# Load order ahead of the last weight-gradient blocks, the shift gradient's row by band products, and a last block in column halves

## The chip, the cores and the metric

The kernel runs on one core of a Trainium2 chip. The metric is device time in microseconds (us) of one execution, taken as the median of several runs. The engines are called PE (matrix products, with PEld for its weight loads), ACT, DVE and POOL (elementwise work, copies, small operations), and SP (issues transfers). Transfers that SP issues form one queue in program order; POOL issues another, and ACT a few.

## What is computed

The program runs a four-layer forward pass and its backward pass, and returns the output and eight gradients. Cut to what the change touches:

```python
def _A_ref(q, k, v, shift_k, ssm_k, ssm_D):      # S=2048, D=448, ks=4
    k_pad = jnp.pad(k, ((0, 0), (ks - 1, 0), (0, 0)))
    for t in range(ks):
        k_shift = k_shift + k_pad[:, t:t + S, :] * shift_k[:, ks - 1 - t][None, None, :]
    kv = k_shift * v
    ...                                            # long convolution of kv with ssm_k, by FFT
    return q * (y + kv * ssm_D)
def _B_ref(x, w1, w2):                             # w1: [448, 1792], w2: [1792, 448]
    h = silu(einsum("bsd,df->bsf", x, w1))
    return einsum("bsf,fd->bsd", h, w2)
x = x + _A_ref(layernorm(x), ...); x = x + _B_ref(layernorm(x), ...)
x = x + _A_ref(layernorm(x), ...); x = x + _B_ref(layernorm(x), ...)
# returned: x, and the gradients of q, k, v, shift_k, ssm_k, ssm_D, w1, w2
```

Three of the gradients matter here. The one of `w2` ([1792, 448], output 8) and the one of `w1` ([448, 1792], output 7) are sums over the 2048 rows and over both dense layers. The one of `shift_k` ([448, 4], output 4) holds, for each of the 448 channels and 4 shifts, one sum over the rows.

## The kernel before

The first 460 us or so run the tiled forward and backward passes. They write to DRAM what the weight gradients need: the activations `A0_d`, `A1_d`, the gradients `GH0_d`, `GH1_d` (one for each of the two dense layers) and the normalised rows `N_d` (two tensors, one for each layer). The rest is class `Tail`: `jobs("w2")`, an FFT stage, `ends` (gradients of k, v, ssm_k, ssm_D and shift_k) and `jobs("w1")`. The work of these parts is interleaved on PE.

**Order.** No engine's order is written by hand. Each step is recorded with `s.op(cost, fn, r, w, prio, ...)`: its guessed cost on each engine it may run on, the tiles that it reads and writes, a priority (lower goes first), for a transfer also kind and bytes, and `behind`, a list of steps after whose issue it may be issued. `Sched.plan` (a list scheduler with guessed rates, `RATE`) turns this into one order for every engine, and the program is emitted in that order. Semaphore waits come from the tiles: a reader waits for the writer, a writer waits for the readers of the buffer that it takes over. The guessed costs and rates only decide order.

**Weight gradients, `jobs`.** The 1792 columns are cut into seven blocks p = 0..6 of 256 columns, each of two halves u = 0, 1 of 128. For a block, both layers' operands (gi = 0, 1) of 16 row tiles are loaded into an operand buffer `jb` [128, 16, 256] of 1024 KB; then each half sums 2 x 16 matmuls (stationary: `jb`, 128x128; moving: 448 columns) into one PSUM tile `ps_d`. There are three `jb` buffers, and for w1 every even block's first operand (p = 0, 2, 4, 6, gi = 0) is kept in the buffer of `Minv` where `(2p + gi) % 4 == 0`; the buffer `Minv` is free when the last `ps_gK` and `ps_gkv` products are done. For `w2` the operand is a plain load from `A0_d`/`A1_d` (L1114); for `w1` it is a transposing load from `GH1_d` and `GH0_d` (L1112), and the moving operand is `nmov`, the rows `N_d[1]` and `N_d[0]`, loaded in two halves each (L1095, 896 KB each). All are issued by SP. In step p = 1 of w1 both halves share one two-bank PSUM tile. A copy `dob` of `ps_d` to SBUF follows (L92 on ACT, L94 on DVE); blocks 0 to 5 are transposed by a transfer (L1191) and stored by POOL (L1208, L1210). Block 6 is transposed by PE (`ps_dt`, L1197, four products per half), copied (`do`), and stored by SP in one transfer (L1212), which ends the program.

The last 2 x 448-column sums of w2 (block 6) come directly before block 0 of w1. The order of SP's queue there is: second-last w2 operand, rows `N_d[1]` (2 loads), last w2 operand, first transposing load of GH1, rows `N_d[0]` (2 loads), second transposing load, and so on.

**Shift gradient, `ends`.** For each group q of 128 channels (64 in the last), 32x128 products `ps_sk` (L1051, two halves h of 8 row tiles) hold on their diagonal the wanted sums. DVE multiplies with an identity (`gsel`, L1061), reduces (`gsk`, L1063, one value per channel and shift) and casts into `gskb` (L1065). PE turns `gskb` into one row on one partition by 16 transposes (`ps_gs`, L1075), ACT copies it in another order (`gsr`, L1079), and POOL stores it (L1080). Interleaved on DVE are the sums `gka`/`gkp` (L1027 to L1036) of the gradient of k, in eight steps g, each stored by POOL (L1039).

Of the kernel before, what the change touches and what calls it, by code (L numbers as in the profile page):

```python
# [20 lines left out]
P = 128  # L21
S = 2048
D = 448
# [109 lines left out]
class Sched:  # L133
# [5 lines left out]
    STEP = 20  # L139
    RATE = {"plain": 300e3, "turn": 160e3, "load": 190e3, "rows": 220e3}  # L140

# [18 lines left out]
    def at(self, base, *key):  # L160
        return base + NUDGE.get(key, 0.0)
# [188 lines left out]
def _pm(ap2d):  # L350
    return ap2d.rearrange("(p j) d -> p j d", j=J)
# [487 lines left out]
class Tail:  # L839
# [119 lines left out]
    def ends(self, pr):  # L959
# [63 lines left out]
        for g in range(8):  # L1023
# [15 lines left out]
            s.op({"POOL": 0.6}, lambda e, gk=gk, g=g: nc.gpsimd.dma_start(out=out2[:, 2 * g:2 * g + 2, :], in_=gk[:]), r=[gk], prio=pr + 5, dma=("plain", 230e3))  # L1039
        gskb = s.vb("P2", "gskb", [P, 4, 4], BF16, "gskb")  # L1040
        prev = []
        for q in range(4):
# [15 lines left out]
            def pick(e, q=q, nb=nb, pd=pd, sel=sel, gsk=gsk):  # L1058
                for b in range(nb):
                    m = k.ident[32 * b:32 * b + 32, 32 * b:32 * b + 32].unsqueeze(1)  # L1060
                    nc.vector.tensor_tensor(out=sel[32 * b:32 * b + 32], in0=pd[32 * b:32 * b + 32], in1=m.to_broadcast([32, 4, 32]), op=ALU.mult)  # L1061
                n = 32 * nb
                nc.vector.tensor_reduce(out=gsk[0:n], in_=sel[0:n], axis=mybir.AxisListType.X, op=ALU.add)  # L1063
                for j in range(4):
                    nc.vector.tensor_copy(gskb[0:n, q, j:j + 1], gsk[0:n, 3 - j:4 - j])  # L1065

            s.op({"DVE": 1.5}, pick, r=[pd], w=[sel, gsk, gskb], prio=pr + 4)

        pg = self.unit([1, 4, D], BF16, "ps_gs")

        def row4(e):
            for q in range(4):
                n = 128 if q < 3 else 64
                for j in range(4):
                    nc.tensor.transpose(pg[0:1, j, 128 * q:128 * q + n], gskb[0:n, q, j:j + 1], k.ident[0:n, 0:n])  # L1075
# [4 lines left out]
        s.op({"POOL": 0.6}, lambda e: nc.gpsimd.dma_start(out=k.outs[4].rearrange("(o d) j -> o (d j)", o=1), in_=gsr[:]), r=[gsr], prio=pr + 4, dma=("plain", 5e3))  # L1080

    def jobs(self, which, pr):
        nc, s, k = self.nc, self.s, self.k
        if which == "w2":
            gm = s.vb("res", "W1", [P, NT, D], BF16, "gmov")
            gs = [gm.sub() for _ in range(4)]
            gl = [lambda i=i: s.op({"SP": 0.4}, lambda e: nc.sync.dma_start(out=gm[:, 4 * i:4 * i + 4, :], in_=_pm(k.grad_out[0])[:, 4 * i:4 * i + 4, :]), w=[gs[i]], prio=pr - 30, dma=("plain", 458e3), behind=[k.lastA_op]) for i in range(4)]
            groups = [("A1", [gs[t // 4] for t in range(NT)], lambda t: gm[:, t, :]), ("A0", k.G2v, lambda t: k.G2[:, t, :])]
        else:
            nm = [s.vb("PF", ("A1", "B1v")[i], [P, NT, D], BF16, "nmov") for i in range(2)]  # L1090
            nh = [[v.sub() for _ in range(2)] for v in nm]
            for i in (1, 0):
                for h in range(2):
                    hs = slice(8 * h, 8 * h + 8)
                    s.op({"SP": 0.4}, lambda e, i=i, hs=hs: nc.sync.dma_start(out=nm[i][:, hs, :], in_=_pm(k.N_d[i][:])[:, hs, :]),  # L1095
                         r=[k.st_[("n", i, j)] for j in range(8 * h, 8 * h + 8)], w=[nh[i][h]], after=self.done[i], prio=pr - 30 if i else pr + 0.5, dma=("plain", 917e3), behind=k.loads[-1 - i:][:1])
            groups = [("GH1", [nh[1][t // 8] for t in range(NT)], lambda t: nm[1][:, t, :]), ("GH0", [nh[0][t // 8] for t in range(NT)], lambda t: nm[0][:, t, :])]
# [29 lines left out]
        else:  # L1127
            for p, gi, at in ((0, 0, pr), (1, 0, pr + 0.2), (0, 1, pr + 1), (1, 1, pr + 2)):
                bring(p, gi, 0, 16, at)
        for p in range(NF // 2):  # L1130
            q = s.at(pr + 12.5 * p, p, which)
# [25 lines left out]
            if (which, p) == ("w1", 1):  # L1157
                prev = first[:4]
            both = True
            steps = [(u, gi) for gi in range(2) for u in range(2)] if both else [(u, gi) for u in range(2) for gi in range(2)]  # L1160
# [3 lines left out]
            for x, (u, gi, ts) in enumerate(split):  # L1164
                ends = [[y for y in range(len(split)) if split[y][0] == u][z] for z in (0, -1)]
# [4 lines left out]
                def mm(e, ts=ts, gi=gi, u=u, rows=rows, ps=pss[u], at=groups[gi][2], first=(x == ends[0]), last=(x == ends[1])):  # L1170
                    for t in ts:
                        nc.tensor.matmul(ps[:, :D], lhsT=rows(t, gi, u), rhs=at(t), start=(first and t == ts[0]), stop=(last and t == ts[-1]))  # L1172

                if (which, p, x) == ("w1", 1, 4):
                    prev = [first[-1], mine[-1]]
                prev = [s.op({"PE": 0.19 * len(ts)}, mm, r=[*[parts[gi][t] or k.lastA for t in ts], *[groups[gi][1][t] for t in ts]], w=[pss[u]], prio=q + 0.05 * x - (12.35 if (which, p) == ("w1", 1) and x < 4 else 0), after=prev + (self.last if p else [k.lastG] if u and which == "w2" else []))]
# [5 lines left out]
            for u in range(2):  # L1182
                ps = pss[u]
# [4 lines left out]
                s.op({"ACT": 0.55, "DVE": 0.62}, lambda e, ps=ps, ob=ob: _copy(nc, e, ob[:], ps[:, :D]), r=[ps], w=[ob], prio=q)  # L1188
# [6 lines left out]
                def tr(e, ob=ob, pt=pt):  # L1195
                    for dc in range(ND):
                        nc.tensor.transpose(pt[:, dc, :], ob[:, dc * DC:(dc + 1) * DC], k.ident[:])  # L1197

                s.op({"PE": 0.25}, tr, r=[ob], w=[pt], prio=q)
                s.op({"ACT": 0.6, "DVE": 0.4}, lambda e, pt=pt, o=o, u=u: _copy(nc, e, o[:, :, u, :], pt[:]), r=[pt], w=[o], prio=q)  # L1200
            if which == "w2":
# [13 lines left out]
def kernel(  # L1215
# [68 lines left out]
    "P1": dict(pq=3, sp=1),  # L1284
    "P2": dict(skb=1, gK=2, gkv=2, gKD=1, sel=2, gsk=2, gskb=1, gKr=1, oo=2, ob=2),
}
# [100 lines left out]
```

## Time and profile before

| what | before |
|---|---|
| median of 3 runs (lowest to highest) | 700.63 us (699.21 to 701.17) |
| the profiled execution: its time | 699.83 us |
| its span, first to last instruction | 698.0 us |
| PE, DVE, ACT, POOL busy in the span | 97%, 73%, 58%, 24% |
| granted PE clock | 1.00 of full speed in every stretch from 566 to 696 us |

PE is close to always busy, so a saving counts when it shortens PE's own sequence, a wait of PE, or the few steps after PE's last product. The chain of waits is read backwards from the last instruction: it names, at each step, what released it. A row of the timeline reads: start, duration, engine, line, operation, tile written and read, shapes, count, and in square brackets how long the engine had stood idle before it and what ended that. For SP and POOL a transfer's row is its issue, not its landing; landings are in the view of transfers.

### The profile page before, as it was taken

Reading aid. Unit: us, or ns where it says so; the run is one execution under the profiler, and the core shown is the slowest. Engines: PE = TensorE matmul, PEld = TensorE weight load, DVE = VectorE, ACT = ScalarE, POOL = GpSimd, SP = SyncE. Lnnn points to the kernel's source line nnn. Section 1 sums busy time; section 2 is a strip of 40 time slices with the busy share of each in tenths; the row PEclk is TensorE's granted clock in tenths of the full one; section 3 lists DMA queues with packets and bytes.
Section 4 is the critical chain, followed back from the end, with each engine's and each line's share of the span. In section 5 each row is a group of like instructions: output and inputs, shape, how many; then the busy total and the mean of one; then the engine's idle time right before and its main releaser. Section 6 shows DMA issues by size and latency. Waiting matters only on the chain. (4 is left out here: it accounts for less than half of the span.)

```text
span 698.0 us, 18012 instructions
## 1 busy us (share of the span) xinstructions
PE 676.8 (97%) x7448; PEld 469.2 (67%) x7464; DVE 512.8 (73%) x1203; ACT 401.8 (58%) x486; POOL 168.2 (24%) x290
## 2 busy tenths in 40 slices
PE   6999898999999999999999999999999999999997
PEld 4887666776767776777767767655767765455553
DVE  5989798668889888888889877864699679951000
ACT  4989987776667556766567666425876550002001
POOL 1254153203222323122212201013143131102221
PEclk9999999999999999999999999999999999999999
DMA  9979988989788978787886769977699679999972
GB/s 320 289 247 291 363 165 181 199 180 190 181 154 180 183 189 181 177 176 187 183 181 143 174 158 237 296 191 231 201 387 350 181 258 302 302 238 219 230 159 46
DMA packets 280671, 151.86 MB, mean 218 GB/s; under 512 B 230159, under 2 KB 261631, under 8 KB 280205
## 3 DMA queue, kind: packets, MB, share of 16 engines
q1 hardware_dynamic: 265854, 108.29, 67.2%
q0 software_dynamic: 13968, 41.62, 19.5%
q8 instruction: 58, 0.95, 0.6%
q10 hardware_dynamic: 766, 0.80, 0.4%
q14 instruction: 25, 0.20, 0.1%
HBM read 50.68 MB, written 54.60 MB: 151 GB/s over the span
## 5 line engine op out<-in xcount | busy, mean ns | idle before, releaser
L1172 PEld LDWEIGHTS <-jb 128*128 128x128 bf16 x892 | 85.8, 98 | 81.6 <-DMA jb<-GH_d 2.0
L92 ACT CAST ghp<-ps_g 128x896 bf16<-128x896 f32 x64 | 58.1, 908 | 58.5 <-PE ps_g L672 48.5
L726 PE MATMUL ps_o<-w2sb,aT 128*128 128x448 bf16 x448 | 89.7, 352 | 0.8 <-ACT aT L700 0.8
L726 PE MATMUL ps_n<-w1T,ghT 128*128 128x448 bf16 x448 | 90.0, 352 | 0.0
L1172 PE MATMUL ps_d<-nmov,jb 128*128 128x448 bf16 x448 | 86.3, 353 | 2.2 <-DMA jb<-GH_d 1.6
L663 PE MATMUL ps_h<-nT,w1sb 128*128 128x128 bf16 x1344 | 85.6, 219 | 0.8 <-ACT nT L92 0.8
L663 PE MATMUL ps_g<-nT,w2T 128*128 128x128 bf16 x1344 | 85.7, 219 | 0.0
L663 PEld LDWEIGHTS <-w2T 128*128 128x128 bf16 x1344 | 77.3, 98 | 7.2
L663 PEld LDWEIGHTS <-w1sb 128*128 128x128 bf16 x1344 | 76.7, 98 | 5.2 <-issue 0.9
L726 PEld LDWEIGHTS <-aT 128*128 128x128 bf16 x448 | 43.0, 98 | 38.4 <-ACT aT L700 1.0
L726 PEld LDWEIGHTS <-ghT 128*128 128x128 bf16 x448 | 43.1, 98 | 37.8
L700 ACT ACTIVATE aT<-ps_h 128x896 bf16<-128x896 f32 x64 | 56.7, 916 | 19.9 <-PE ps_h L672 11.0
L622 POOL TENSOR_TENSOR rstd<-ve,mhalf 128x1 f32<-128x1 f32 x64 | 39.3, 614 | 106.6 <-DVE ve L619 106.6
L700 ACT ACTIVATE dT<-ps_h 128x896 bf16<-128x896 f32 x60 | 53.3, 915 | 14.9 <-PE ps_h L672 10.0
L750 DVE SCALAR_TENSOR_TENSOR junk<-u,n 128x448 bf16<-128x448 bf16 x64 | 39.9, 624 | 23.2 <-ACT u L829 22.2
L92 ACT CAST dob<-ps_d 128x448 bf16<-128x448 f32 x13 | 6.9, 532 | 70.9 <-PE ps_d L1172 70.9
L700 ACT ACT_TABLE_LOAD x36 | 46.2, 1283 | 1.2 <-issue 0.6
L1172 PE MATMUL ps_d<-G,jb 128*128 128x448 bf16 x224 | 45.7, 353 | 0.1
L1172 PE MATMUL ps_d<-gmov,jb 128*128 128x448 bf16 x220 | 45.1, 352 | 0.0
L617 DVE BATCH_NORM_STATS2 st<-x 128x6 f32<-128x448 bf16 x64 | 40.0, 625 | 1.5
L739 DVE TENSOR_TENSOR ghT<-ghp,dT 128x896 bf16<-128x896 bf16 x64 | 39.4, 620 | 1.1 <-ACT ghp L92 0.9
L829 ACT ACTIVATE u<-ps_n,rstd 128x448 bf16<-128x448 f32 x32 | 20.3, 636 | 32.3 <-POOL rstd L622 13.8
(180 smaller groups left out, 1218.2 us busy)
## 6 DMA issues: line engine op xcount, KB each, us to landing
A_d<-turned SPq DMA_DIRECT2D x32, 448.0 KB, 4.0
GH_d<-ghT SPq DMA_DIRECT2D x32, 448.0 KB, 4.1
jb<-A_d SPq DMA_DIRECT2D x12, 1024.0 KB, 6.7
KK<-KK POOLq DMA_DIRECT2D x14, 256.0 KB, 5.1
spec_K<-KK POOLq DMA_DIRECT2D x7, 512.0 KB, 6.0
spec_KV<-X POOLq DMA_DIRECT2D x7, 512.0 KB, 7.7
N_d<-n POOLq DMA_DIRECT2D x32, 112.0 KB, 4.0
sp_c<-spec_KV POOLq DMA_DIRECT2D x14, 256.0 KB, 6.6
```

Source lines behind the costliest of these rows:

```text
L92: nc.scalar.copy(out, in_)
L617: nc.vector.bn_stats(out=st[:], in_=x[:])
L622: s.op({"POOL": 1.0}, lambda e: nc.gpsimd.tensor_tensor(out=rs[:], in0=ve[:], in1=self.k.mhalf[:, 0:1], op=ALU.pow), r=[ve], w=[rs], prio=pr)
L663: nc.tensor.matmul(ps[:, i, :], lhsT=at(b, ft), rhs=nT[:, b, :], **f)
L700: prev = [s.op({"ACT": 0.93}, lambda e, i=i, fun=fun, out=out, late=late: nc.scalar.activation(out[:, 7 * i:7 * i + 7, :], c[:, 7 * i:7 * ...
L726: nc.tensor.matmul(po[:, :D], lhsT=a[:, ft, :], rhs=wt[:, ft * D:(ft + 1) * D], start=(ft == 0), stop=(ft == NF - 1))
L739: s.op({"DVE": 0.57}, lambda e, i=i, t=t: nc.vector.tensor_tensor(out=gh[:, 7 * i:7 * i + 7, :], in0=t[:], in1=d[:, 7 * i:7 * i + 7, :], o ...
L750: nc.vector.scalar_tensor_tensor(out=junk[:], in0=u[:], scalar=1.0, in1=n[:], op0=ALU.mult, op1=ALU.mult, accum_out=cp[:, 1:2])
L829: s.op({"ACT": 0.85}, lambda e: nc.scalar.activation(u[:], pn[:, :D], ACT.Identity, scale=r[:], accum_out=cp[:, 0:1]), r=[pn, r], w=[u, cp ...
L1172: nc.tensor.matmul(ps[:, :D], lhsT=rows(t, gi, u), rhs=at(t), start=(first and t == ts[0]), stop=(last and t == ts[-1]))
```

## The change

There are three edits, and one changed guess of a rate in the planner.

1. **Order of the loads** (`jobs("w1")`). The first transposing load of GH1 (p = 0, gi = 0) gets priority `pr - 60` and goes behind the second-last operand of w2 instead of behind the last; the row loads of both `N_d[1]` and `N_d[0]` go behind the last operand of w2; the other transposing loads go behind that one too.
2. **Shift gradient**. Two constant tiles are made on POOL (`spread`: four 32x32 identities below each other; `band`: ones in four bands). DVE spreads each channel's four sums over 32 columns (`gskx`, four multiplications of 128x32 per group instead of four casts of 128x1). Four matmuls with `band` as stationary operand sum them into a [14, 128] tile, in place of the 16 transposes; ACT copies that tile, and POOL stores 14 lines of 256 bytes instead of one row.
3. **The last block of w1** (p = 6). Half u = 1 is cut into two column halves of 224 with a PSUM tile each; copy, PE transposes and copy are done for each of the two (two `ps_dt` products instead of four).

In the built program, the order on PE before the last blocks changes too: the second half of the `ps_sk` products of group 1 moves from the middle of w2's block 6 to the middle of w1's block 0, the two `ps_sk` steps of group 3 move to within the last products of w1's block 1 and between the halves of block 2, and the four band products come after the first layer's products of block 2. On DVE the copy of one `ps_d` half at 641 us goes to ACT; on POOL the store of w2's block 6 moves ahead of the fourth `gkp` store. SP's queue becomes: second-last w2 operand, first transposing load of GH1, last w2 operand, rows `N_d[1]`, rows `N_d[0]`, second transposing load, and so on.

The diff, cut to its core:

```diff
-    RATE = {"plain": 300e3, "turn": 160e3, "load": 190e3, "rows": 220e3}
+    RATE = {"plain": 300e3, "turn": 160e3, "load": 215e3, "rows": 220e3}
...
+        spread = s.vb("P2", "m32", [P, 32], BF16, "gsm")
+        band = s.vb("P2", "band", [P, 4, 16], BF16, "gsl")
+        def masks(e):
+            nc.gpsimd.memset(band[:], 0.0)
+            for b in range(4):
+                nc.gpsimd.memset(band[32 * b:32 * b + 32].rearrange("p q r -> p (q r)")[:, b:b + 61:20], 1.0)
+                nc.gpsimd.tensor_copy(spread[32 * b:32 * b + 32], k.ident[32 * b:32 * b + 32, 32 * b:32 * b + 32])
+        s.op({"POOL": 1.5}, masks, w=[spread, band], prio=pr)
+        gskx = s.vb("P2", "gK", [P, 4, 32, 4], BF16, "gskx")
...
                 for j in range(4):
-                    nc.vector.tensor_copy(gskb[0:n, q, j:j + 1], gsk[0:n, 3 - j:4 - j])
+                    nc.vector.tensor_scalar(out=gskx[0:n, q, :, j], in0=spread[0:n], scalar1=gsk[0:n, 3 - j:4 - j], scalar2=None, op0=ALU.mult)
...
-        pg = self.unit([1, 4, D], BF16, "ps_gs")
-        def row4(e):
+        pg = self.unit([14, P], FP32, "ps_gs")
+        def lines(e):
             for q in range(4):
                 n = 128 if q < 3 else 64
-                for j in range(4):
-                    nc.tensor.transpose(pg[0:1, j, 128 * q:128 * q + n], gskb[0:n, q, j:j + 1], k.ident[0:n, 0:n])
+                nc.tensor.matmul(pg[:], lhsT=band[0:n, q, 0:14], rhs=gskx[0:n, q].rearrange("p e j -> p (e j)"), start=(q == 0), stop=(q == 3))
-        s.op({"PE": 1.0}, row4, r=[gskb], w=[pg], prio=pr + 4)
+        s.op({"PE": 0.25}, lines, r=[gskx, band], w=[pg], prio=pr + 4)
-        gsr = s.vb("P2", "gK", [1, D * 4], BF16, "gsr")
-        s.op({"ACT": 1.8}, lambda e: nc.scalar.copy(gsr[:].rearrange("o (d j) -> o j d", j=4), pg[:]), r=[pg], w=[gsr], prio=pr + 4)
+        gsr = s.vb("P2", "gsr", [14, P], BF16, "gsr")
+        s.op({"ACT": 0.2}, lambda e: nc.scalar.copy(gsr[:], pg[:]), r=[pg], w=[gsr], prio=pr + 4)
...
-            for i in (1, 0):
+            def rows_of(i, behind):
                 for h in range(2):
                     hs = slice(8 * h, 8 * h + 8)
...
-                         r=[k.st_[("n", i, j)] for j in range(8 * h, 8 * h + 8)], w=[nh[i][h]], after=self.done[i], prio=pr - 30 if i else pr + 0.5, dma=("plain", 917e3), behind=k.loads[-1 - i:][:1])
+                         r=[k.st_[("n", i, j)] for j in range(8 * h, 8 * h + 8)], w=[nh[i][h]], after=self.done[i], prio=pr - 30, dma=("plain", 917e3), behind=behind)
+            rows_of(1, k.loads[-1:])
+            rows_of(0, k.loads[-1:])
+            second = k.loads[-1]
+            k.load = k.loads[-2:-1]
...
-            for p, gi, at in ((0, 0, pr), (1, 0, pr + 0.2), (0, 1, pr + 1), (1, 1, pr + 2)):
+            for p, gi, at in ((0, 0, pr - 60), (1, 0, pr + 0.2), (0, 1, pr + 1), (1, 1, pr + 2)):
                 bring(p, gi, 0, 16, at)
+                if (p, gi) == (0, 0):
+                    k.load = [second]
...
+            cols = [(0, 0, D), (1, 0, D)]
+            if (which, p) == ("w1", NF // 2 - 1):
+                cols = [(0, 0, D), (1, 0, D // 2), (1, D // 2, D)]
+                pss.append(self.unit([P, 512], FP32, "ps_d"))
             if split is None:
-                split = [(u, gi, range(8 * h, 8 * h + 8)) for u, gi in steps for h in range(2)]
+                split = [(v, gi, range(8 * h, 8 * h + 8)) for gi in range(2) for v in range(len(cols)) for h in range(2)]
...
-                        nc.tensor.matmul(ps[:, :D], lhsT=rows(t, gi, u), rhs=at(t), start=(first and t == ts[0]), stop=(last and t == ts[-1]))
+                        nc.tensor.matmul(ps[:, c0:c1], lhsT=rows(t, gi, u), rhs=at(t)[:, c0:c1], start=(first and t == ts[0]), stop=(last and t == ts[-1]))
...
-                pt = self.unit([DC, ND, P], BF16, "ps_dt")
+                ds = range(c0 // DC, c1 // DC)
+                pt = self.unit([DC, len(ds), P], BF16, "ps_dt")
                 def tr(e, ob=ob, pt=pt, ds=ds):
-                    for dc in range(ND):
-                        nc.tensor.transpose(pt[:, dc, :], ob[:, dc * DC:(dc + 1) * DC], k.ident[:])
+                    for i, dc in enumerate(ds):
+                        nc.tensor.transpose(pt[:, i, :], ob[:, dc * DC:(dc + 1) * DC], k.ident[:])
```

More of the change, by code (lines that the diff above doesn't have):

```diff
@@ L1163, in jobs, with mm @@
             mine = []
-            for x, (u, gi, ts) in enumerate(split):
-                ends = [[y for y in range(len(split)) if split[y][0] == u][z] for z in (0, -1)]
+            for x, (v, gi, ts) in enumerate(split):
+                u, c0, c1 = cols[v]
+                ends = [[y for y in range(len(split)) if split[y][0] == v][z] for z in (0, -1)]
                 def rows(t, gi, u, p=p, early=early, st=st):
                     return k.lastA[:, 2 * p + u, :] if early and which == "w2" and (gi, t) == (0, 15) else st[gi][:, t, u * P:(u + 1) * P]
-                def mm(e, ts=ts, gi=gi, u=u, rows=rows, ps=pss[u], at=groups[gi][2], first=(x == ends[0]), last=(x == ends[1])):
+                def mm(e, ts=ts, gi=gi, u=u, rows=rows, ps=pss[v], c0=c0, c1=c1, at=groups[gi][2], first=(x == ends[0]), last=(x == ends[1])):
@@ L1181, in jobs @@
                 prev = [first[-1], mine[-1]]
-            for u in range(2):
-                ps = pss[u]
+            for v, (u, c0, c1) in enumerate(cols):
+                ps = pss[v]
                 if which == "w2":
@@ L1284 @@
     "P1": dict(pq=3, sp=1),
-    "P2": dict(skb=1, gK=2, gkv=2, gKD=1, sel=2, gsk=2, gskb=1, gKr=1, oo=2, ob=2),
+    "P2": dict(skb=1, gK=2, gkv=2, gKD=1, sel=2, gsk=2, m32=1, band=1, gsr=1, gKr=1, oo=2, ob=2),
 }
```

20 lines of the change are left out of this document (9 added, 11 removed).

## The prediction

> **What bounds the kernel now.** First I read the page: PE is busy nearly all of the span.
>
> ```profile
> span 698.0 us, 18012 instructions
> ...
> PE 676.8 (97%) x7448; PEld 469.2 (67%) x7464; DVE 512.8 (73%) x1203; ACT 401.8 (58%) x486; POOL 168.2 (24%) x290
> ```
>
> So a saving must shorten PE's own sequence, one of its waits, or the steps after its last product. All three edits act after 575 us, and in the built program every engine's order before that point is unchanged except for nine small POOL operations. Next I read the chain of waits in order of time from there on (start, duration, what):
>
> ```profile
> 594.54 14.78 DMA jb<-GH_d
> 609.36 1.69 PE ps_d L1172 x8
> ...
> 627.55 0.54 ACT dob L92
> 628.14 1.67 PE ps_d L1172 x8
> ...
> 638.70 0.96 PE ps_gs L1075 x16
> 639.66 51.56 PE ps_d L1172 x272
> ...
> 691.44 1.53 PE ps_d L1172 x8
> 692.99 0.54 ACT dob L92
> 693.58 0.45 PE ps_dt L1197 x4
> 694.05 0.42 DVE do L94
> ```
>
> Between 594 and 692 us PE loses time in two places only, and PE's timeline has their size in the brackets:
>
> ```profile
> 609.36 1.69 PE L1172 MATMUL ps_d<-nmov,jb 128*128 128x448 bf16 x8 [1.61 <-DMA jb<-GH_d]
> ...
> 628.14 1.67 PE L1172 MATMUL ps_d<-nmov,jb 128*128 128x448 bf16 x8 [0.62 <-ACT dob L92]
> ```
>
> PE waits 1.61 us for the second transposing load of GH1 and 0.62 us for a copy of half a block. After 628 it never waits until 693. At most about 2.2 us of waits, 1 us of `ps_gs` and a part of the end are to be had: a large gain is not there.
>
> **Edit 1, the order of the loads.** SP's queue and the landings of single issues:
>
> ```profile
> 574.85 0.52 SPq L1114 DMA_DIRECT2D jb<-A_d  x1
> 575.60 2.25 SPq L1095 DMA_DIRECT2D nmov<-N_d  x2
> 581.57 0.52 SPq L1114 DMA_DIRECT2D jb<-A_d  x1
> 582.27 11.07 SPq L1112 DMA_TRANSPOSE jb<-GH_d  x1
> 593.44 1.01 SPq L1095 DMA_DIRECT2D nmov<-N_d  x2
> 594.54 10.90 SPq L1112 DMA_TRANSPOSE jb<-GH_d  x1
> ...
> 631.91 4.76 SPq L1112 DMA_TRANSPOSE jb<-GH_d  x1
> ```
>
> ```profile
> jb<-A_d SPq DMA_DIRECT2D x1, 1024.0 KB, 10.4
> ...
> jb<-GH_d SPq DMA_TRANSPOSE x1, 14.8
> ```
>
> The load that PE waits for is issued at 594.54 and lands 14.8 later, at 609.3. In the changed order its issue can come at about 588 (its buffer is free when PE has used up the second operand of w2's block 5). But an earlier issue helps only if the DMA engines would otherwise idle. These are the windows (PE, PEld, DVE, ACT, POOL busy, clock, DMA share, GB/s):
>
> ```profile
> 582.00:584.00 2.00, 2.00 (x12) 1.02 (x11) 1.97 (x3) 0.00 (x0) 0.00 (x0) 1.00 0.99 409
> ...
> 590.00:592.00 2.00, 2.00 (x41) 1.07 (x40) 1.97 (x4) 0.00 (x0) 0.33 (x1) 1.00 1.19 100
> 592.00:594.00 2.00, 2.00 (x12) 1.06 (x11) 2.00 (x4) 0.00 (x0) 0.23 (x1) 1.00 1.27 290
> ...
> 598.00:600.00 2.00, 2.00 (x12) 1.02 (x11) 1.88 (x9) 0.53 (x1) 0.00 (x0) 1.00 1.07 421
> ...
> 602.00:604.00 2.00, 2.00 (x13) 0.99 (x12) 1.97 (x3) 0.27 (x1) 0.71 (x1) 1.00 0.74 82
> ```
>
> From 578 to 609 the engines are full, with two thin places, at 590 to 592 and 602 to 604: in each a transposing load comes to the head of the queue, and for some 1.5 us little flows. Between the issue at 574.85 and the landing at 609.3 the queue carries eight loads (two w2 operands, four halves of rows, two transposing loads); in the changed order the same eight stand up to and including the second transposing load, and two transposing loads still follow plain ones. So I expect its landing to move little. What does change is a POOL store. Here are the fourth `gkp` store and the store of w2's block 6:
>
> ```profile
> 596.95 0.54 POOL L1039 DMA_DIRECT2D out_dram<-gkp  x1 [4.71 <-DVE gkp L1036]
> 602.56 0.71 POOL L1202 DMA_DIRECT2D out_dram<-do  x1 [5.08 <-ACT do L92]
> ```
>
> They change places, so the 224 KB that were issued at 596.95 leave after 603; at 421 GB/s they take 0.5 us out of the way of the awaited load. PE needs it at the same point as before (same products ahead of it). The wait goes from 1.6 to 1.1: **-0.5**. Bounds: -1.6 (the wait vanishes, if the first load's thin 1.5 us falls behind the plain load then still in flight) and +2.8 above the present wait (the rival below).
>
> The first transposing load is moved past the last w2 operand and the rows `N_d[1]`, and holds SP meanwhile: its issue took 11.07 with four loads in front, and one such issue took 4.76 at 631.91 where none was. With one load in front I take about 8.5, an estimate from the flow: the plain load in front needs until about 580 (1024 KB at some 300 GB/s from 576.5), the transposing load some six more (a thin 1.5 us, then 1024 KB at the 290 of the window from 592, and a store), and SP is released some 2 us before the last of it (it was at 593.34, while the rate of rows comes after 595). So SP is free at 584, not 582. The last w2 operand then goes out about 2.5 us later and, with the 10.4 from issue to landing, lands by 594.5; PE asks for it at 594.8. The rows `N_d[1]`, needed at 601, go out 10 us later than now and land by about 597. Both stay hidden, the first barely. `N_d[0]` is needed at 616 only.
>
> **The order on PE.** The 0.62 wait comes from step p = 1, whose halves share one PSUM tile: the last eight products wait for the copy of the first half. In the changed order the 16 `ps_sk` products of group 3 stand between, and they cost the same anywhere:
>
> ```profile
> 629.81 0.55 PE ps_sk L1051 x16
> ```
>
> 0.55 of the 0.62 is covered: **-0.55** (bounds 0, if the products are held by the same copy, and -0.62). The second `ps_sk` step of group 1 moves from 596.4 to about 604.4. DVE's next step needs it:
>
> ```profile
> 598.26 1.19 DVE L1061 TENSOR_TENSOR gsel<-ps_sk,ident 32x128 f32<-32x128 f32 x4
> ...
> 635.61 0.57 DVE L1061 TENSOR_TENSOR gsel<-ps_sk,ident 32x128 f32<-32x128 f32 x2 [6.95 <-PE ps_sk L1051]
> ```
>
> DVE stands idle some 6 us there, and the four sums g = 4 to 7 queue behind it (also their stores). It has room: it stood idle 6.95 before the last `gsel`. That step then ends at about 634, while PE needs its result at about 636, 16 products after the last `ps_sk`. If DVE were another 6 us late, PE would wait 4; I take 0.
>
> **Edit 2, the band products.** Sixteen transposes take 0.96 on PE, in the chain. Four products of 128 columns take their place. The nearest rows are `ps_gK` with 128 columns and its own weights, and the transposes themselves:
>
> ```profile
> 558.37 0.89 PE ps_gK L1002 x16
> ```
>
> 0.89/16 = 0.056, 0.96/16 = 0.060: four cost 0.22 to 0.24. **-0.73**. On DVE four multiplications of 128x32 replace four casts; bounds are the casts and the 112x112 form:
>
> ```profile
> L414 DVE TENSOR_SCALAR KK<-ident,skc 112x112 bf16<-112x112 bf16 x16 | 2.6, 246 | 5.2 <-POOL skc L408 5.2
> ...
> L1065 DVE CAST gskb<-gsk 128x1 bf16<-128x1 f32 x12 | 1.0, 149 | 0.1
> ```
>
> At most 4 x 0.1 = 0.4 us per group, in the room just named. ACT's copy gets shorter, off the path. POOL's nine operations on the masks fall in its idle 9 us before the first `gK` store; at 0.1 to 0.3 each they need 1 to 3:
>
> ```profile
> 555.17 0.57 POOL L1007 DMA_DIRECT2D out_dram<-gK  x1 [9.04 <-ACT gK L92]
> ```
>
> ```profile
> L407 POOL MEMSET KK<- 112x32 bf16 x2 | 0.4, 300 | 0.0
> ```
>
> **Edit 3, the end.** 32 products of 448 columns become 64 of 224. Per product 51.56/272 = 0.190 in the chain for 448 columns and 0.056 for 128: on a straight line 0.096 for 224, so 64 x 0.096 - 32 x 0.190 = +0.1 (bounds 0 and +6, if a half cost as much as a whole; the 128-column row with its own weights excludes most of that). The Trainium skill (TensorE: Matmul & The Clock Gate, Part 1) puts a warm product at its columns over 2.4 GHz plus 2.5 ns, which is 95.8 ns here; by it the sum would be the same to 0.1. Two transposes more stand before the last products: +0.1. Behind them, ACT's copy shrinks from 448 to 224 columns:
>
> ```profile
> 560.21 0.91 ACT L985 CAST gkv<-ps_gkv 128x896 bf16<-128x896 f32 x1
> ...
> 689.79 0.53 ACT L92 CAST dob<-ps_d 128x448 bf16<-128x448 f32 x1 [8.59 <-PE ps_d L1172]
> ```
>
> 0.38 for 448 columns more, so 0.34 for 224: -0.19. Two transposes instead of four: 0.45 to 0.34, -0.11. The last copy has 256 columns on ACT (0.15 + 0.22 = 0.37) instead of 512 on DVE (0.42): -0.05. Sum of the end: **-0.15** (bounds -0.35 and +0.2).
>
> **Sum.** -0.5 - 0.55 - 0.73 - 0.15 = -1.9 us. The profiled execution took 699.83 (span 698.0 and 1.8 around it), so 697.9 in its frame. The three timed runs have the median 700.63, 0.8 above it; the mean of all four is 700.2. I subtract from that: 698.3, and say 698.4.
>
> **The rivals.**
> (a) The wait vanishes. For it: the thin 1.5 us of the first transposing load may fall under the plain load in front of it, and the store leaves the window. Against it: in both places before, plain loads were in flight too, and it was not hidden. -1.6 instead of -0.5: -3.0, 697.2.
> (b) Slower. The place is SP at 575.5: if the moved load holds SP for 11.07, as it did at 582.27, the last w2 operand is issued at 586.5, 5 us late, and lands at 596.9 (10.4 after issue); PE, which wants it at 594.8, waits 2.1. All loads behind are 5 late, so the second transposing load lands at 613.8 against a need at 609.9 and PE waits 3.9. Waits of 6.0 instead of 1.6 (+4.4), less the 1.4 of the other edits: +3.0, 703.2. It decides when SP is held beyond 584.4 (594.8 - 10.4), an issue of 9 us. For it: both issues quoted took 11. Against it: those had rows of 1.8 MB and more in front, this one has 1 MB. The Trainium skill (Advanced Engine Details and Errata, X-Bar Transpose (TRN2)) says that transposing transfers are as fast as plain ones; by it this rival could not arise and its chance would be nil, but the rows of 11.07 and 0.52 for the same 1024 KB do not agree.
> (c) The order does not do what it says: the landing stays, and the `ps_sk` products are held with the copy. Only -0.73 - 0.15 remain: -0.9, 699.3.
>
> **How the numbers follow.** Forecast 0.47, (a) 0.31, (b) 0.08, (c) 0.14. About 0.3% (2.1 us) is what a measurement of this kernel can tell from no change. The forecast's -1.9 lies just inside; with its own spread of about 1, I give 0.4 of it to faster. Faster: 0.31 + 0.19 = 0.50. Slower: most of (b), 0.06. Within: 0.44. The forecast's own range is 697.3 to 699.6; (a) and (c) and the spread of the runs (about 1 either way) widen it to 696.5 and 700.8, which leaves (b) out.
>
> **What would show it.** In the changed profile: PE's wait for `jb<-GH_d` near 608 of about 1 us (0: rival a; a wait at 594.8 before the `jb` of w2 as well: b); the first transposing issue at 575.5 holding SP 7 to 9 us; no PE wait over 0.2 for `dob` near 627; `ps_gs` x4 in about 0.25; from the last `ps_d` product to the last issue 1.25 us instead of 1.55 (692.99 to 694.5). I am wrong if PE waits anywhere for DVE's `gskx`, or if the 64 half products take over 6.3 us.

## The result and the profile after

| | before | after |
|---|---|---|
| median of the timed runs | 700.63 us (9 runs) | 698.38 us (9 runs) |
| ratio of after to before, 95% interval | | 0.9972 (0.9959 to 0.9986) |
| the profiled execution: its time, its span | 699.83, 698.0 us | 696.9, 695.1 us |

The changed kernel is 0.28% faster. The two profiled executions differ by 2.9, but 1.04 of that is there before the change acts: the second-last w2 operand is issued at 574.85 before and at 573.81 after. What is compared from here on is the **stretch** from that issue to the issue of the last output: 119.69 before (574.85 to 694.54), 117.84 after (573.81 to 691.65), so **-1.85**.

The chain of waits of the changed kernel (start, duration, what) where it differs:

```profile
607.89 1.69 PE ps_d L1192 x8
...
626.08 0.54 ACT dob L92
...
635.05 0.41 PE ps_gs L1084 x4
635.46 53.13 PE ps_d L1192 x304
...
688.82 0.77 PE ps_d L1192 x8
...
690.50 0.35 ACT dob L92
690.90 0.33 PE ps_dt L1219 x2
691.25 0.37 ACT do L92
```

`ps_gs` has shrunk from 0.96 to 0.41, and the steps behind the last product are 0.35, 0.33 and 0.37 long instead of 0.54, 0.45 and 0.42. PE's timeline at the two former waits:

```profile
607.89 1.69 PE L1192 MATMUL ps_d<-nmov,jb 128*128 128x448 bf16 x8 [1.18 <-DVE gka L1035]
...
625.98 0.62 PE L1061 MATMUL ps_sk<-kx_s,gks 128*32 128x128 bf16 x16
626.66 4.70 PE L1192 MATMUL ps_d<-nmov,jb 128*128 128x448 bf16 x24
```

The wait for the second transposing load is still there, 1.18 instead of 1.61. The bracket names a DVE step, because its end fell beside the landing. SP's queue and the landing show the true one: issue at 588.43, landing 19.4 later, at 607.8.

```profile
573.81 0.52 SPq L1129 DMA_DIRECT2D jb<-A_d  x1
574.55 7.68 SPq L1127 DMA_TRANSPOSE jb<-GH_d  x1
582.33 0.53 SPq L1129 DMA_DIRECT2D jb<-A_d  x1
583.04 5.30 SPq L1105 DMA_DIRECT2D nmov<-N_d  x4
588.43 15.32 SPq L1127 DMA_TRANSPOSE jb<-GH_d  x1
```

```profile
jb<-GH_d SPq DMA_TRANSPOSE x1, 19.4
```

(Where a run without the early stores, e6 below, has the same DVE step end at 609.7, PE passes this place at 608.5 without a wait: it doesn't wait for DVE.) At 626 the 16 `ps_sk` products fill the time of the copy `dob`: they end at 626.60, the copy at 626.62, and no bracket is left. The first moved load held SP for 7.68. DVE's two late steps:

```profile
603.63 1.19 DVE L1071 TENSOR_TENSOR gsel<-ps_sk,ident 32x128 f32<-32x128 f32 x4 [5.47 <-PE ps_sk L1061]
...
633.03 0.69 DVE L1075 TENSOR_SCALAR gskx<-gsm,gsk 64x32 bf16<-64x32 bf16 x4
```

DVE stood idle 5.47, and its last `gskx` was done at 633.7, 1.3 ahead of PE's use at 635.05. On POOL the two stores have changed places:

```profile
600.86 0.71 POOL L1224 DMA_DIRECT2D out_dram<-do  x1 [9.24 <-ACT do L92]
601.56 0.57 POOL L1039 DMA_DIRECT2D out_dram<-gkp  x1
```

The fourth `gkp` store landed at 607.4, 0.4 ahead of the second transposing load; before, it was issued at 596.95 and landed at 604.3, 5 ahead of that load.

### The profile page after: what moved, and what is told of

It is laid out like the page before. It is cut to its first block, busy times and chain, and to the rows that moved or that the text cites. A ratio compares the mean times of both kernels' runs of the same rounds, so it can differ in the third digit from the quotient of the medians.

```text
span 695.1 us, 18061 instructions
## 1 busy us (share of the span) xinstructions
PE 675.2 (97%) x7468; PEld 471.5 (68%) x7484; DVE 513.6 (74%) x1202; ACT 398.8 (57%) x489; POOL 169.5 (24%) x299
## 5 line engine op out<-in xcount | busy, mean ns | idle before, releaser
L1192 PEld LDWEIGHTS <-jb 128*128 128x128 bf16 x924 | 88.9, 98 | 77.9 <-DMA jb<-GH_d 1.6
L1192 PE MATMUL ps_d<-nmov,jb 128*128 128x448 bf16 (+1 forms) x480 | 86.5, 340 | 1.3 <-DVE gka L1035 1.2
L92 ACT CAST dob<-ps_d 128x448 bf16<-128x448 f32 (+1 forms) x15 | 7.6, 507 | 74.7 <-PE ps_d L1192 74.7
```

What stands on the lines that cost most here:

```text
L92: nc.scalar.copy(out, in_)
L1192: nc.tensor.matmul(ps[:, c0:c1], lhsT=rows(t, gi, u), rhs=at(t)[:, c0:c1], start=(first and t == ts[0]), stop=(last and t == ts[-1]))
```

## The experiments

The runs by the stretch and what PE lost in it (T2 is the wait for the second transposing load; "copy" is the half-block copy at 627; "other" are waits for other loads; "clock" is what products took longer while the granted PE clock was 0.50, explained at e4; the rest is the stretch less these). e5 moves the issue at which the stretch starts and is left out.

| kernel | stretch | T2 | copy | other | clock | rest |
|---|---|---|---|---|---|---|
| before | 119.69 | 1.61 | 0.62 | - | - | 117.46 |
| after | 117.84 | 1.18 | - | - | - | 116.66 |
| e9, after again, timed | 117.87 | 1.21 | - | - | - | 116.66 |
| e8, after again | 120.21 | 1.95 | - | - | 1.59 | 116.67 |
| e7, bands in reverse | 117.84 | 1.17 | - | - | - | 116.67 |
| e1, old order | 120.16 | 2.88 | 0.62 | - | - | 116.66 |
| e2, old order, one store less | 119.26 | 0.95 | 0.62 | 0.85 | - | 116.84 |
| e3, new order alone | 118.16 | 0.61 | - | - | - | 117.55 |
| e4, rows `N_d[0]` late | 123.99 | - | - | 4.63 | 2.80 | 116.56 |
| e6, after, four stores less | 116.50 | - | - | - | - | 116.50 |
| e10, rows `N_d[1]` first | 117.75 | - | 0.62 | 0.43 | - | 116.70 |
| e11, both rows first | 124.89 | - | - | 5.54 | 2.70 | 116.65 |
| e12, half of them first | 117.98 | 1.43 | - | - | - | 116.55 |

This table is the main reading. With bands and halves the rest is 116.5 to 116.8 in eleven profiles, without them 117.46 and 117.55: edits 2 and 3 are worth 0.8 to 0.9 wherever they stand. All else is waits, and in three runs the clock after a wait. Edit 1 moves only those.

### e1: the old order, bands and halves kept

```diff
-            rows_of(1, k.loads[-1:])
-            rows_of(0, k.loads[-1:])
-            second = k.loads[-1]
-            k.load = k.loads[-2:-1]
+            for i in (1, 0):
...
-                         ... prio=pr - 30, dma=("plain", 917e3), behind=behind)
+                         ... prio=pr - 30 if i else pr + 0.5, dma=("plain", 917e3), behind=k.loads[-1 - i:][:1])
...
-            for p, gi, at in ((0, 0, pr - 60), (1, 0, pr + 0.2), (0, 1, pr + 1), (1, 1, pr + 2)):
+            for p, gi, at in ((0, 0, pr), (1, 0, pr + 0.2), (0, 1, pr + 1), (1, 1, pr + 2)):
```

(The planner's rate is 190 again, too.)

> The order of the loads and of PE's work as in the kernel before; the band products and the column halves kept. The stretch counted is the one from the issue of the second-last w2 operand to the issue of the last output: 119.7 us before (574.85 to 694.54), 117.8 after (573.81 to 691.65). Theory: edit 1 gave two things, about 0.44 at the wait for the second transposing load and about 0.66 at the copy of the half block. Both waits come back (1.6 and 0.6) and the stretch is 118.9. Rival: the landing is free and PE's order gave nothing; the stretch stays within 0.2 of 117.8.

Measured: median 700.93, ratio to before 1.0008 (0.9992 to 1.0024). Both waits are back in PE's timeline, the first larger than before:

```profile
611.31 1.69 PE L1185 MATMUL ps_d<-nmov,jb 128*128 128x448 bf16 x8 [2.88 <-DMA jb<-GH_d]
630.08 1.67 PE L1185 MATMUL ps_d<-nmov,jb 128*128 128x448 bf16 x8 [0.62 <-ACT dob L92]
```

The 0.62 is the order's doing: it is in before, e1, e2 and e10, where the last products of step p = 1 follow the others at once, and in none of the runs with `ps_sk` products between them. The first wait is 2.88 against 1.61 with the same order of loads, a difference of 1.27 and so larger than the 0.43 between before and after. The two programs differ a little there: the longer `gskx` step delays the fourth `gkp` store from 22.1 to 22.5 after the second-last w2 operand. Whether that or chance makes the 1.27 is not shown.

### e2: the same, without the fourth gkp store

```diff
-            ... lambda e, gk=gk, g=g: nc.gpsimd.dma_start(out=out2[:, 2 * g:2 * g + 2, :], in_=gk[:]) ...
+            ... lambda e, gk=gk, g=g: g != 3 and nc.gpsimd.dma_start(out=out2[:, 2 * g:2 * g + 2, :], in_=gk[:]) ...
```

> As e1, and the fourth gkp store is left out (two rows of that output stay unwritten). Theory: the awaited load lands when the bytes ahead of it are through, and edit 1 shortened the wait only because it moved this 224 KB store behind the load. With the old order and no store, the wait is 1.1 instead of 1.6, and the stretch 118.4. Rival: the store costs the load nothing, and the earlier issue did it; the wait stays at 1.6, the stretch at 118.9.

Measured (one execution): the wait is 0.95. Windows of e1, then of e2 (PE, PEld, DVE, ACT, POOL busy, clock, DMA share, GB/s):

```profile
602.00:604.00 2.00, 2.00 (x12) 1.06 (x11) 2.00 (x3) 0.53 (x1) 0.72 (x1) 1.00 0.28 70
604.00:606.00 2.00, 2.00 (x13) 0.99 (x11) 1.97 (x4) 0.00 (x0) 0.47 (x1) 1.00 1.18 186
606.00:608.00 2.00, 2.00 (x12) 1.08 (x11) 2.00 (x4) 0.00 (x0) 0.10 (x1) 1.00 1.24 211
```

```profile
602.00:604.00 2.00, 2.00 (x12) 1.00 (x11) 2.00 (x3) 0.53 (x1) 0.67 (x1) 1.00 0.45 103
604.00:606.00 2.00, 2.00 (x12) 1.08 (x11) 1.97 (x4) 0.00 (x0) 0.45 (x2) 1.00 1.28 290
606.00:608.00 2.00, 2.00 (x13) 1.00 (x11) 2.00 (x4) 0.00 (x0) 0.17 (x1) 1.00 1.12 301
```

In both runs the load starts with some 2 us in which little flows (70 and 103). From 604 to 606 the load runs alone in e2, at 290; in e1, where POOL had issued the fourth `gkp` store at 598.02, 0.14 of the 0.37 MB moved are that store's, and all together flow at 186. From 606 to 608 the windows tell less: in e2 0.23 of the 0.60 MB are the `do` store's, and in e1 the flow is thin (211) though hardly any store bytes are left (0.01 MB). The wait went where the theory said: 1.9 less than in e1, 0.7 less than in before, whose order is the same. But those two, both with the store, are 1.27 apart, so this one execution does not price the store. The bytes alone would be 0.8 at 290; e6 below prices it better. Part of the gain came back as a wait of 0.85 for the next transposing load.

### e3: the new order alone

```diff
-            if (which, p) == ("w1", NF // 2 - 1):
+            if False:
...
-                nc.tensor.matmul(pg[:], lhsT=band[0:n, q, 0:14], ... )
+                for j in range(4):
+                    nc.tensor.transpose(pg[0:1, j, 128 * q:128 * q + n], gskb[0:n, q, j:j + 1], k.ident[0:n, 0:n])
```

> Only the order is changed; sixteen transposes for the shift row and the whole last block as before. Theory: the waits are those of the changed kernel (1.2 for the load, none over 0.2 for the copy), ps_gs takes 0.96 in the chain instead of 0.41, and from the last product on it takes 0.2 more: the stretch is 118.6. Rival: the order's gain needs the band products (the longer ps_gs or ACT's copy moves a wait); the stretch is 119.2 or more.

Measured: median 699.81, ratio 0.9984 (0.9974 to 0.9994); stretch 118.16. The copy is covered, `ps_gs` takes 0.96 again, and the wait for the load is

```profile
609.74 1.69 PE L1183 MATMUL ps_d<-nmov,jb 128*128 128x448 bf16 x8 [0.61 <-DMA jb<-GH_d]
```

The stretch is 0.4 under the expectation because this wait is 0.6 shorter, and the rest is 117.55 where 117.4 was expected. Edit 1 needs nothing of the other two.

### e4: rows N_d[0] behind the second transposing load

```diff
-            rows_of(0, k.loads[-1:])
...
                 bring(p, gi, 0, 16, at)
+                if (p, gi) == (1, 0):
+                    rows_of(0, k.loads[-1:])
```

> The changed kernel, with the two halves of the rows N_d[0] issued behind the second transposing load instead of ahead of it. Theory: the load lands when the bytes ahead of it are through; 1792 KB less at the 300 to 400 GB/s of these windows are 4.5 to 6 us, so it lands by 603.5 in the changed kernel's frame, the wait of 1.18 vanishes, and the stretch is 116.7, if PE does not wait for the third transposing load or N_d[0] instead (they then land about 611 to 614, against a need near 609 to 614: up to 2 us are given back). Rival: the landing is bound to the transposing load's own pace (its hold on SP and its start), and comes at most 1 us earlier; the wait is 0.2 to 1.2 and the stretch 117 to 118.

Measured: median 702.56, ratio 1.0019 (1.0000 to 1.0038), stretch 123.99. The wait for the second load is gone, and PE stands at the third:

```profile
620.06 9.02 PE L1193 MATMUL ps_d<-nmov,jb 128*128 128x448 bf16 x32 [4.63 <-DMA jb<-GH_d]
```

The 32 products also take 9.02 instead of 6.2. They did not wait: in windows of 1 us the granted PE clock is 0.50 from 619 to 625, after PE had stood idle 4.63, and 1.00 again from 626. So the wait cost 2.8 on top of itself. The third load was issued at 601.82 and landed 18.2 later, against an expected 611 to 614: a miss of 6 us. In the changed kernel the third load has the same bytes in front of it on SP's queue and lands 37.4 after the second-last w2 operand, here 44.8.

### e5: the first transposing load ahead of both last w2 operands

```diff
-            k.load = k.loads[-2:-1]
+            k.load = k.loads[-3:-2]
```

> The changed kernel, with the first transposing load ahead of both last w2 operands instead of ahead of one. Its buffer is free at about 571, when the DMA engines are half idle (154 to 302 GB/s in 570 to 574 and 51 in 574 to 576 in the changed kernel). Theory: what stands behind it leaves about 2 us earlier, so the second transposing load lands before PE asks for it and the wait of 1.18 is gone; from the second-last group of ps_sk before the rows to ps_gs (583.45 to 634.98 there, 51.5) it is 50.4, and the time about 697.2. Rival: the load's hold on SP makes the second-last w2 operand late (issued after 576 instead of 573.8), PE waits for it near 587 by up to 3 us, and the time is 699 or more.

Measured: median 701.80, ratio 1.0017 (1.0003 to 1.0031). The rival holds. SP's queue and PE:

```profile
572.49 8.30 SPq L1127 DMA_TRANSPOSE jb<-GH_d  x1
580.89 4.64 SPq L1129 DMA_DIRECT2D jb<-A_d  x2
```

```profile
589.64 1.69 PE L1192 MATMUL ps_d<-gmov,jb 128*128 128x448 bf16 x8 [0.99 <-DMA jb<-A_d]
...
611.53 3.20 PE L1192 MATMUL ps_d<-nmov,jb 128*128 128x448 bf16 x16 [2.22 <-DMA jb<-GH_d]
```

The load held SP for 8.30 although little stood in front of it on SP's queue (POOL had issued its stores of `gK`, 448 KB, at 572.08 and `ksf`, 224 KB, at 572.63), and the second-last w2 operand went out 7 us later than in the changed kernel.

### e6: the changed kernel without its first four gkp stores

```diff
-            ... lambda e, gk=gk, g=g: nc.gpsimd.dma_start(out=out2[:, 2 * g:2 * g + 2, :], in_=gk[:]) ...
+            ... lambda e, gk=gk, g=g: g > 3 and nc.gpsimd.dma_start(out=out2[:, 2 * g:2 * g + 2, :], in_=gk[:]) ...
```

> The changed kernel without the first four gkp stores (eight rows of that output stay unwritten). With the old order, leaving out the fourth store took the wait from 2.88 to 0.95. Theory: a store that runs beside a transposing load costs it more than its own bytes (224 KB at 290 GB/s would be 0.8), so without the fourth, which is issued at 601.56 while the load's data come, the load lands 1 to 2 us earlier, the three others give some 0.5 each, and the wait of 1.18 is 0. Rival: the thin spots of the load itself set its landing; the wait stays at 0.6 or more.

Measured (one execution): 697.41; no wait for a load, stretch 116.50. The load landed at 605.8, 30.1 after the issue of the second-last w2 operand; in after, e7 and e9 it was 34.0 to 34.1, in e3 33.4 and in e8 34.8. Four stores less, 896 KB, brought it 3.3 to 4.7 earlier: 0.8 to 1.2 for each on the average, against the 0.5 of the prediction. Three of the four landed by 597.0 in after, so they ran beside the loads ahead of it; only the fourth ran in the awaited load's own time.

### e7: the four bands in reverse order

```diff
-            for q in range(4):
+            for q in (3, 2, 1, 0):
...
-                ... start=(q == 0), stop=(q == 3))
+                ... start=(q == 3), stop=(q == 0))
```

> The changed kernel with the four band products in reverse order, so that the first waits for the last of DVE's results and the other three need no wait of their own. Theory: ps_gs took 0.41 instead of 0.23 because three of its four products carry a wait on DVE's semaphore; with one wait it takes 0.22 to 0.28 in the chain. Rival: a product with fresh weights and 14 rows out costs 0.10 whatever it waits for; it stays at 0.38 to 0.43.

Measured (one execution): 698.67. The chain of waits:

```profile
636.50 0.41 PE ps_gs L1084 x4
```

The rival's size holds: the waits cost nothing. But the price is not 0.10 for each product. Short windows of the changed kernel's timeline show their starts:

```profile
634.98 0.22 PE L1084 MATMUL ps_gs<-gskx,gsl 128*14 128x128 bf16 x1
635.04 0.42 PE L1084 MATMUL ps_gs<-gskx,gsl 128*14 128x128 bf16 x3
635.25 0.22 PE L1084 MATMUL ps_gs<-gskx,gsl 64*14 64x128 bf16 x1
635.40 0.36 PE L1192 MATMUL ps_d<-nmov,jb 128*128 128x448 bf16 x1
```

The third starts at 635.10. So two steps take 0.06 each, as the prediction had it, and two take 0.15: the one to the product of group 3, whose weights have 64 rows, and the one from it to the 128x128 weights of `ps_d`. In e7 the 64-row product comes first (starts 636.42, 636.57, 636.63, 636.69, then `ps_d` at 636.84), and again the two long steps are where the shape of the weights changes. The 16 transposes before have such steps too: 0.15 to the 64-row ones (639.24 to 639.39) and 0.12 back to `ps_d` (639.47 to 639.59), where 64-row ones follow each other at 0.03. No run changes the shape alone, so that the shape is the cause is a reading of these rows.

### e8 and e9: the changed kernel again, with no edit

> The changed kernel once more, to see how far its wait for the second transposing load goes from one execution to the next. Theory: the wait was 1.18 and, in the kernel with the order alone, 0.61; here it lies between 0.3 and 1.5, while ps_gs (0.41) and the wait at the copy of the half block (none) repeat to 0.05. Rival: it repeats to 0.1 at 1.18, and the 0.61 came from the edits that e3 lacks.

> The changed kernel again, timed beside the kernel before. The single look at it took 702.0 with waits of 3 us for the second transposing load, the nine earlier runs 696.9 to 699.8. Theory: the wait for that load moves between 0.6 and 3 from run to run, the other terms (copy of the half block 0.66, ps_gs 0.55, end 0.2 to 0.3) are fixed; the median is 698 to 700, 1.0 to 2.5 under before, and the spread 4 us or more. Rival: 702 was an accident of that one execution; the median is 698.4 within 0.6.

Measured: e8 702.02, with a stretch of 120.21. PE waits 1.95 for the load, outside the expected 0.3 to 1.5, and then runs at half the clock for a while (PE's row, then windows of 1 us):

```profile
611.10 2.87 PE L1192 MATMUL ps_d<-nmov,jb 128*128 128x448 bf16 x8 [1.95 <-DMA jb<-GH_d]
```

```profile
612.00:613.00 1.00, 1.00 (x4) 0.35 (x3) 1.00 (x3) 0.00 (x0) 0.26 (x1) 0.50 1.27 290
...
615.00:616.00 1.00, 1.00 (x6) 0.49 (x5) 0.97 (x2) 0.00 (x0) 0.00 (x0) 1.00 1.16 251
```

The eight products take 2.87 instead of 1.69 and the 32 `ps_sk` products 1.04 instead of 0.63: 1.59 lost to the clock. e9: median 698.83, 696.9 to 699.6 in 12 runs, ratio 0.9971 (0.9960 to 0.9981), and 1.21 at the load. The gain repeats on another occasion with the same size. The spread of its runs, 2.7, is under the expected 4, and its median fits the rival too; e8 is above all 21 timed runs of this kernel.

### e10, e11, e12: more of the rows ahead

```diff
-            rows_of(1, k.loads[-1:])
+            rows_of(1, k.loads[-3:-2])
```

(e11: also `rows_of(0, k.loads[-2:-1])`; e12: only the first half, `behind=k.loads[-3:-2] if i and not h else behind`, and the rate at 205.)

> The changed kernel, with the two halves of the rows N_d[1] (1792 KB) issued ahead of the second-last w2 operand, as soon as their buffer is free (about 570.5), into the stretch where the DMA engines are half idle (51 to 302 GB/s in 570 to 576). Unlike the transposing load moved there in e5 they do not hold SP long (two took 2.25 before). Theory: all that stands behind leaves 2 to 3 us earlier, the second transposing load lands before PE asks for it, PE waits for no load over 0.3 us after 583, and the median is 1 to 2 us under that of e9. Rival: the second-last w2 operand (needed at about 588) lands late behind 1792 KB, or the gain goes to a wait for the third transposing load; the median is that of e9 or above.

> As e10, and the rows N_d[0] moved ahead of the last w2 operand as well. Theory: bytes that leave earlier are bytes that no longer stand ahead of the transposing loads, but the last w2 operand, needed at about 595, now stands behind 1792 KB more and the first transposing load: it lands at 594 to 597, so PE waits 0 to 2 us for it, and the median is that of e10 to 2 us above. Rival: all loads are early enough; the median is that of e10 within 0.5.

> The changed kernel, with only the first half of the rows N_d[1] (896 KB) ahead of the second-last w2 operand (and the planner's assumed rate of the transposing loads at 205 instead of 215, which keeps ps_sk products between the halves of step p = 1). In e10 both halves ahead took the wait for the second transposing load away, but SP was held 11.51 by the first one (7.83 in e9), so PE waited 0.43 for the last w2 operand, and 0.62 came back at the copy of the half block. Theory: SP's hold goes with the bytes in front, so it is about 9.5 here; the last w2 operand is in time (no wait over 0.1 near 595), the second transposing load lands 1 to 2 us earlier than in e9, the wait of 1.21 is 0 to 0.3, the copy stays covered, and the median is 0.5 to 1.2 under e9's 698.83. Rival: the hold is 11 as soon as rows stand in front of the load, and PE waits for the last w2 operand; the median is that of e10 (699.0) or above.

Measured: e10 699.02, ratio 0.9985 (0.9961 to 1.0009); e11 705.45, 1.0071 (1.0057 to 1.0085); e12 699.08, 0.9977 (0.9963 to 0.9991). None beats the changed kernel. SP's hold by the first transposing load, in e12, e10 and e11:

```profile
574.93 9.76 SPq L1127 DMA_TRANSPOSE jb<-GH_d  x1
```

```profile
575.87 11.51 SPq L1127 DMA_TRANSPOSE jb<-GH_d  x1
587.48 0.54 SPq L1129 DMA_DIRECT2D jb<-A_d  x1
```

```profile
575.79 11.23 SPq L1127 DMA_TRANSPOSE jb<-GH_d  x1
```

With one load of 1024 KB in front the hold is 7.68 (7.83 in e9), with 896 KB of rows besides 9.76, with 1792 KB 11.2 to 11.5: it grows by 1.5 to 2 us for each 0.9 MB in front, as e12's theory said. e5's 8.30, with little in front on this queue, is not on that line. What waits behind it shows in PE's timeline of e10, and worse of e11:

```profile
595.06 6.23 PE L1192 MATMUL ps_d<-G,jb 128*128 128x448 bf16 x32 [0.43 <-DMA jb<-A_d]
...
627.27 3.19 PE L1192 MATMUL ps_d<-nmov,jb 128*128 128x448 bf16 x16 [0.62 <-ACT dob L92]
```

```profile
600.09 7.41 PE L1192 MATMUL ps_d<-G,jb 128*128 128x448 bf16 x24 [5.54 <-DMA jb<-A_d]
```

In e10 the load was in time, and the gain went into these two waits. In e11 the last w2 operand landed at 600.0 instead of the expected 594 to 597, and behind the wait of 5.54 the clock was 0.50 again until 605, for another 2.7. In e12 the last w2 operand was in time too, but the second transposing load was no earlier:

```profile
609.08 10.77 PE L1192 MATMUL ps_d<-nmov,jb 128*128 128x448 bf16 x56 [1.43 <-DMA jb<-GH_d]
```

The theory failed there. Its DMA windows of 1 us show why the 896 KB that left early did not help:

```profile
599.00:600.00 1.00, 1.00 (x7) 0.49 (x5) 0.96 (x2) 0.00 (x0) 0.00 (x0) 1.00 0.73 68
...
602.00:603.00 1.00, 1.00 (x36) 0.62 (x25) 0.97 (x4) 0.00 (x0) 0.00 (x0) 1.00 1.27 188
603.00:604.00 1.00, 1.00 (x7) 0.54 (x6) 0.94 (x4) 0.00 (x0) 0.00 (x0) 1.00 1.12 140
...
605.00:606.00 1.00, 1.00 (x8) 0.50 (x6) 1.00 (x2) 0.00 (x0) 0.00 (x0) 1.00 0.06 7
```

The load's data came earlier, from 598 on, and lost the lead: to its start, to low flow at 602 to 604 beside the `gkp` store that POOL issued at 595.43 and that landed at 604.2, and to 1 us at 605 in which next to nothing moves.

## Why the prediction was right

The sum was -1.9, the stretch gave -1.85, and the median was 698.38. That it came so close is in part luck: the terms' errors cancel, and the wait in the first term moves by more from run to run than it was to shrink. By its steps:

- **The wait for the second transposing load, -0.5.** It went from 1.61 to 1.18 (-0.43). Right were that the landing moves little (34.5 after the issue of the second-last w2 operand before, 34.0 after) although the issue comes 5 us earlier, that the fourth store moves its bytes later, and that stores count (e6). Mis-sized was the price of a store: 0.5 was taken, e6 gives 0.8 to 1.2. That the wait shrank by less all the same fits with thin windows that the load has in the changed kernel with no store beside it (78 and 112 GB/s at 602 to 604, shown below). The step also left out how far this wait moves between runs: 0.61 to 1.95 in five profiles of the new order (after, e3, e7, e8, e9), 1.61 and 2.88 in two of the old, and that a wait can halve the clock behind it (e4, e8, e11). So the 0.43 is the difference of one pair of executions, not a settled size, and that the store's new place caused it is argued from e2 and e6, not shown.
- **The order on PE, -0.55.** Right: the 0.62 is covered in every profile with `ps_sk` products between the halves, and back in e1. From the second load's first product to `ps_gs` it is 29.34 before and 27.16 after, which lacks eight products (1.52) there: 0.66 less.
- **The band products, -0.73.** Direction right, size wrong: 0.96 to 0.41, so -0.55. The term "four cost 0.22 to 0.24" was mis-sized: it took 0.06 for every step, but two of the four steps, where the shape of the weights changes, take 0.15 (e7). Dividing 0.96 by 16 had spread such steps over sixteen products. The waits on DVE are not the cause (e7).
- **The end, -0.15.** From the end of `ps_gs` to the last issue it is 54.88 before and 56.19 after, which has eight whole products more in this part (8 x 0.190 = 1.52): 56.40 to 56.19, so -0.2. The half products took 0.77/8 = 0.096, as forecast. The errors of the four terms are +0.07, -0.11, +0.18 and -0.05, which is why the sum held.
- **SP's hold, about 8.5, and what lies behind.** 7.68; the last w2 operand was issued at 582.33 and landed by 590.9, ahead of PE's use at 593.8.

The rivals: (a) needs more than the moved store; the wait vanishes in e6, where all four stores are gone. (b) did not come, but its mechanism is real: in e10 and e11 SP was held 11.2 and more, the last w2 operand came late, and PE stood 0.43 and 5.54. It needs 1.8 MB of rows in front, as the argument against it said; e10 got off lightly because the operand then landed in 7.5, not 10.4. The two holds of SP that the prediction compared, 11.07 and 0.52, say nothing of how fast the bytes flow; that is 290 against 416 GB/s (below). (c) is refuted by e3.

**What stays open.** By their whole times, e1 (1.0008) and e3 (0.9984) do not add up to 0.9972. The waits of their profiles account for it (2.88 in e1), but with one profile each it isn't settled whether e1's program always waits that long. Its profiled time, 700.94, is the median of its ten (700.93), which speaks for it; the 696.9 of after is the lowest of its nine.

## What to carry to other kernels

Read a change's worth from a stretch between two fixed instructions, less the waits in it: here the rest repeated to 0.35 us while whole times of one kernel scattered by 3 and more. Look at the granted clock behind a wait before you call slow products a second wait. Before a transposing load is moved, count what stands in front of it and behind it on its queue: with 1 to 2.8 MB in front it held the queue for 7.5 to 11.5 us, and what was queued behind went late. Count the stores of another queue that run ahead of an awaited load or beside it; here four of them delayed it by about 1 us each, twice what their bytes would take.

## What was not expected of the hardware

A transposing load that runs alone flows at 290 GB/s, plain loads before it at 416. Windows of e6:

```profile
597.00:598.00 1.00, 1.00 (x7) 0.53 (x6) 1.00 (x2) 0.00 (x0) 0.00 (x0) 1.00 1.00 416
...
601.00:602.00 1.00, 1.00 (x7) 0.50 (x6) 0.00 (x0) 0.14 (x1) 0.00 (x0) 1.00 1.27 290
602.00:603.00 1.00, 1.00 (x8) 0.50 (x6) 0.00 (x0) 0.40 (x1) 0.31 (x1) 1.00 1.28 290
```

And it is not smooth: it starts with 1 to 2 us of low flow after plain loads, and can have a second such stop in its midst, 7 GB/s at 605 in e12, and in the changed kernel, with no store's bytes beside it, this one:

```profile
602.00:603.00 1.00, 1.00 (x10) 0.35 (x12) 0.00 (x0) 0.00 (x0) 0.13 (x1) 1.00 2.12 78
603.00:604.00 1.00, 1.00 (x36) 0.71 (x36) 0.36 (x2) 0.00 (x0) 0.00 (x0) 1.00 0.52 112
```

What stops it no run here isolates. The Trainium skill (DMA: Bandwidth & Descriptors, Latency and other measured facts) gives 261 GB/s for a transposing transfer with a non-contiguous middle dimension and 350 to 400 for a contiguous one; 290 lies between. The Trainium skill's rule that a transpose next to ordinary transfers "needs nothing" (DMA: Bandwidth & Descriptors, Rules for kernel authors) is about correct results; e6 shows that the neighbours have a price in time.

A wait of PE can cost more than itself. The granted clock fell to 0.50 for some 3.4 us behind the 1.95 of e8, and for some 6.8 us behind the 4.63 of e4 and the 5.54 of e11 (sums of the windows), which lost another 1.59, 2.80 and 2.70. Behind the 2.88 of e1 and the 2.22 of e5 it stayed at 1.00, so the length of the wait alone does not decide it; what does, no run here isolates.
